# Half-array tiles for every attention product: a windowed attention and an MoE layer on one core

## The chip, the core and the metric

The kernel runs on one core of a Trainium2 chip. Five engines work side by side, each with its own queue, in the order in which the program lists their instructions: TensorE (PE in the profile; its weight loads are shown as PEld) multiplies matrices into PSUM, VectorE (DVE) and ScalarE (ACT) do the element work and empty PSUM, GpSimd (POOL) only clears buffers here, and SyncE (SP) issues the DMAs. Engines wait for each other through semaphores. The metric is the device time of one execution in microseconds (us); lower is better.

## The reference

There are 8 batches of 8 heads with head size 64. Each head has 512 local queries and 32 global ones. A local query sees the 32 global keys and the local keys at most 32 places away; a global query sees all 544 keys. The outputs of the heads, side by side, are the rows of a matrix of 4608 x 512, which goes through two products with a squared ReLU between them. All numbers are float32.

```python
    s_g = scale * np.matmul(q_g, k_all.transpose(0, 1, 3, 2))
    out_g = np.matmul(sm(s_g), v_all)
    s_ll = np.where(mask, s_ll, -1000000000.0)      # mask: |i - j| <= 32
    s_l = np.concatenate([s_lg, s_ll], axis=-1)
    out_l = np.matmul(sm(s_l), np.concatenate([v_g, v_l], axis=2))
...
    h = np.maximum(x @ w_in, 0.0)
    return (h * h @ w_out).astype(np.float32)
```

## The kernel before

**Steps.** The work is cut into 128 half heads `t` (8 batches, two halves of the 512 local queries, 8 heads) and 17 blocks of 256 rows of the MoE layer, each block in 8 steps `m`. One loop over `t` runs both: in pass `t` the attention of half head `t` and the MoE step `m = t - LAG` with `LAG = 9`. From pass 137 on there is MoE work alone. A profile line of nearly every instruction is L52, the line of the helper `InOrder` that records it; tiles' names tell them apart. `InOrder` keeps an engine's instructions in the order of the program from the pass that `FREE` names (17 for DVE, ACT and PE); before that pass the Tile scheduler chooses.

**Precision.** The MoE layer and the half heads from 16 on must keep nearly float32 precision while using the type fp32r, so operands are split into a high part (rounded to fp32r by an ACT copy) and the rest (a DVE subtraction), and a product is the sum of three: high x high, high x low, low x high. Those are `x_h, x_l`, `ws` (weights), `gh, gl`, `hi, lo` (keys, queries and values), `ph, pl` (probabilities). The first 16 half heads and the first MoE block are "plain": unsplit float32 products.

**Attention of a half head.** `load_head` brings one packed tile `raw` with keys, queries and values. Each array row pair holds the head's 64 dimensions twice, so that `scores` can use all 128 rows: rows 0 to 63 hold high parts and rows 64 to 127 low parts of the keys, and two products per query tile give the three terms. `softmax1` (DVE: mask, row maximum), `softmax2` (ACT: two exponentials) and `softmax3` (DVE: reciprocal, scaling) make the probabilities of two query tiles of 128 queries by 224 keys. `transposes` turns them by four 128-wide PE transposes into one PSUM bank `pt`; `pt_split` (four ACT copies) and `pt_rest` (three DVE subtractions) make `ph` and `pl`; `av` multiplies them with the values in nine products of 64 output columns into `xa`; `x_evac` writes `x_h` (ACT) and `x_l` (DVE).

**Global attention.** `g_scores` adds one product per half head for the 32 global queries; for each pair of heads the `jobs` table places softmax, transposes (`g_tr`, into `gt`), the split and 13 products (`g_av`, into `gxo`).

**MoE step.** `gemm1(m, 0)` and `gemm1(m, 1)` are 24 products of 256 columns into the PSUM tile `h`, `act1` is a ReLU on ACT and a square on DVE (`r`), `act2` splits it into `gh` (ACT) and `gl` (DVE), and in the next pass `gemm2(m-1)` is 12 products of 512 columns into `o0` and `o1`. When a block is complete, `evac` copies both with ACT into `ot`, from which they are stored, and the next block starts to write `o0` and `o1`. PSUM has 8 banks: two for `h` in turn, two for `o0, o1`, one each for `s`, `pt`, `xa`, `gs`.

**The order of a pass**: transposes of `t-1`; scores of `t`; first half of gemm1; on ACT `pt_split(t-1)`; softmax1 and softmax2 of `t`; `pt_rest(t-1)`; `evac`; second half of gemm1; `av(t-1)`; `g_scores(t)`; `softmax3(t)`; `act1`; `x_evac`; `split_head(t+1)`; gemm2 of `m-1`; `act2`. So DVE finds `pt_rest` between the mask work and `softmax3`, and `x_l`, `lo` and two `hi` subtractions between the square and `gl`.

## Time and profile before

| | |
|---|---|
| runs of the kernel | 1084.47, 1085.22, 1085.70 us (median 1085.22) |
| profiled execution, first to last instruction | 1083.8 us |
| busy: PE, PEld, DVE, ACT | 98%, 87%, 83%, 67% of the span |
| granted TensorE clock | 0.999 |
| one batch in the middle (16 passes, 339.2 to 463.2 us) | 124.0 us, with DVE busy 111.59 and ACT 87.88 |
| HBM | 86.51 MB read, 8.91 MB written |

The profile shows one execution. Its span is 1.4 us below the median of the runs, so sums made against the span are raised by 1.4 us for the runs. Ends of matmuls are modelled and overlap, so the duration of a row does not say what the matmul costs in a stream; the distance between the starts of two rows does. A batch has two half heads of eight heads and comes back every 124.0 us from about 178 us to about 960 us; before that lies the start with the weights' arrival and the plain heads, after it MoE work alone.

### The profile page before, as it was taken

To read this page: it belongs to the slowest core of one execution; us is meant where nothing else is said; L and a number is where in the kernel's file an instruction comes from. 1 tells how busy PE (TensorE), PEld (TensorE's weight loads), DVE (VectorE), ACT (ScalarE), POOL (GpSimd) and SP (SyncE) were. 2 spreads that over 40 slices of the span, in tenths; PEclk is the share of its full clock that TensorE was granted. 3 is DMA by queue.
4 is the path that set the end of the run, shared out by engine and by line. 5 is a ranking of instruction groups with operands and counts; after the bars stand their busy time and mean duration, and the time that the engine had idled before them with its cause. 6 is when DMAs were issued, how large, how long until landed. Compare 5 with 4: busy or idle time off the path is not lost.

```text
span 1083.8 us, 21401 instructions
## 1 busy us (share of the span) xinstructions
PE 1064.4 (98%) x7648; PEld 941.8 (87%) x7648; DVE 894.2 (83%) x2765; ACT 730.4 (67%) x1887; POOL 2.9 (0%) x10
## 2 busy tenths in 40 slices
PE   7999999999999999999999999999999999999998
PEld 5766789998999899988899989998999889998887
DVE  4689998999889898898989899898989899884322
ACT  5889767767677766767677776767677676773322
POOL 0000000000000000000000000000000000000000
PEclk9999999999999999999999999999999999999999
DMA  9933222222222231322222222222222222211000
GB/s 350 357 138 141 82 81 77 87 70 84 82 79 72 84 93 54 100 73 92 62 88 77 76 78 81 77 88 82 81 72 82 68 97 64 86 31 43 2 20 20
DMA packets 55770, 96.81 MB, mean 89 GB/s; under 512 B 6384, under 2 KB 30704, under 8 KB 55664
## 3 DMA queue, kind: packets, MB, share of 16 engines
q1 hardware_dynamic: 55664, 95.44, 27.1%
q8 instruction: 61, 1.00, 0.4%
q14 instruction: 45, 0.37, 0.1%
HBM read 86.51 MB, written 8.91 MB: 88 GB/s over the span
## 4 chain that ended last, share of the span: by engine, by line
PE 83%; DVE 9%; ACT 5%; issue 1%; DMA 1%; SPq 0%; ACTq 0%
PE o L52 31%; PE h L52 31%; PE xa L52 7%; PE s L52 5%; PE pt L52 5%; PE gxo L52 2%; PE gs L52 2%; DVE prob L52 2%; PE gt L52 1%; DVE ph L52 1%; ACT ph L52 1%; ACT prob L52 1%; DVE ws L52 1%; ACT ws L52 1%; DVE st L52 1%
## 5 line engine op out<-in xcount | busy, mean ns | idle before, releaser
L52 PE MATMUL h<-x_h,ws 128*128 128x256 f32 x2048 | 389.3, 283 | 0.0
L52 PEld LDWEIGHTS h<-x_h,ws 128*128 128x128 f32 x2048 | 327.2, 191 | 0.6
L52 PE MATMUL o<-ws,gh 128*128 128x512 f32 x1024 | 321.3, 395 | 0.0
L52 PE MATMUL h<-x_l,ws 128*128 128x256 f32 x1024 | 289.2, 282 | 0.1
L52 PEld LDWEIGHTS o<-ws,gh 128*128 128x128 f32 x1024 | 185.4, 188 | 34.7
L52 PE MATMUL o<-ws,gl 128*128 128x512 f32 x512 | 202.5, 395 | 0.0
L52 PEld LDWEIGHTS h<-x_l,ws 128*128 128x128 f32 x1024 | 196.0, 191 | 0.8 <-DVE x_l L52 0.4
L52 ACT CAST ph<-pt 128x256 fp32r<-128x256 f32 x448 | 141.1, 341 | 57.9 <-PE pt L52 48.7
L52 ACT ACTIVATE prob<-prob,st 128x224 f32<-128x224 f32 x270 | 127.7, 476 | 75.0 <-DVE st L52 72.4
L52 ACT ACTIVATE r<-h 128x512 f32<-128x512 f32 x136 | 81.5, 600 | 100.5 <-PE h L52 99.5
L52 DVE TENSOR_TENSOR r<-h,r 128x512 f32<-128x512 f32 x128 | 88.6, 692 | 63.4 <-ACT r L52 60.8
L52 PEld LDWEIGHTS o<-ws,gl 128*128 128x128 f32 x512 | 96.2, 188 | 22.9
L52 DVE CUSTOM_DVE_ANT_0 prob<-s,con 128x224 f32<-128x224 f32 x256 | 89.8, 387 | 30.9 <-PE s L52 23.7
L52 ACT CAST hi<-raw 128x864 fp32r<-128x864 f32 x112 | 102.4, 915 | 1.3
L52 DVE TENSOR_TENSOR gl<-r,gh 128x512 fp32r<-128x512 f32 x128 | 88.1, 688 | 12.0 <-ACT gh L52 9.9
L52 PE MATMUL xa<-ph,hi 128*64 128x128 f32 x448 | 89.2, 239 | 1.8 <-DVE ph L52 1.2
L52 ACT CAST gh<-r 128x512 fp32r<-128x512 f32 x128 | 79.1, 618 | 16.0 <-DVE r L52 14.7
L52 DVE TENSOR_TENSOR hi<-raw,hi 64x352 fp32r<-64x352 f32 x224 | 82.6, 369 | 6.9
L52 DVE TENSOR_TENSOR ph<-pt,ph 64x128 fp32r<-64x128 f32 x224 | 79.7, 356 | 7.0
L52 PE MATMUL pt<-con,prob 128*128 128x128 f32 (+1 forms) x512 | 79.5, 278 | 0.0
L52 DVE TENSOR_TENSOR lo<-raw,hi 128x448 fp32r<-128x448 f32 x112 | 69.6, 621 | 7.1 <-ACT hi L52 2.7
L52 DVE TENSOR_SCALAR prob<-prob,st 128x224 f32<-128x224 f32 x242 | 70.6, 334 | 4.1
(76 smaller groups left out, 1549.5 us busy)
## 6 DMA issues: line engine op xcount, KB each, us to landing
raw<-in_pk_dram SPq DMA_DIRECT2D x127, 432.0 KB, 3.2
wr<-in_w_dram SPq DMA_DIRECT2D x32, 512.0 KB, 7.3
gv<-in_vg_dram SPq DMA_DIRECT2D x32, 320.0 KB, 3.6
out_dram<-ot SPq DMA_DIRECT2D x32, 256.0 KB, 2.1
qr<-in_qg_dram SPq DMA_DIRECT2D x28, 64.0 KB, 2.7
out_dram<-ot SPq DMA_DIRECT2D x8, 64.0 KB, 1.7
raw<-in_pk_dram SPq DMA_DIRECT2D x1, 304.0 KB, 2.9
con<-in_consts_dram SPq DMA_DIRECT2D x1, 288.0 KB, 4.7
```

The lines of the kernel that those rows point to most:

```text
L52: r = method(*args, **kwargs)
```

## The change

**Half-array tiles.** Keys and queries of the two query tiles are packed into the two halves of the rows: rows 0 to 63 hold the queries of tile 0 with its 224 keys, rows 64 to 127 those of tile 1. Every score product, probability transpose and global transpose now uses 64 rows of the array, and two such instructions, one per half, follow each other and write to different banks (`sb0, sb1` and `pt0, pt1`). The value products use all rows and 64 of the columns: two heads follow each other, and write to the two halves of the partitions of `xa`.

**Unsplit values.** `av` is float32 without a split: three products per half head, issued for two half heads every second pass. `ph`, `pl`, the three DVE subtractions and three of the four ACT copies are gone; `pt_evac` is one copy of 256 columns on ACT (`pt0`) and one on DVE (`pt1`). `split_head` splits 352 columns in place of 864, in one ACT copy and one DVE subtraction. `x_evac` works on 128 partitions every second pass.

**Global attention for four heads at once**, float32 unsplit: ten transposes, four copies out of PSUM, ten products, where two pairs of heads had ten transposes, 26 products and the splits. The score columns of the global queries now lie in the score banks, and are copied and added on 32 partitions in two or three pieces for each half head.

**Order.** PE keeps the written order from the first pass (`FREE`). In a pass, `av` of a pair, global products, `transposes(t-1)` and the scores of `t+1` come first, then all of gemm1 and gemm2. On DVE and ACT, `softmax3(t)` and `split_head(t+2)` come ahead of the mask work of `t+1`. The tile `h` has one bank.

The core of the diff (DRAM layouts, the removed functions and lines that only follow are left out):

```diff
-FREE = (17, 17, 17)
+FREE = (17, 17, 0)
...
-    ps_h = ctx.enter_context(tc.tile_pool(name="ps_h", bufs=2, space=PSUM))
+    pp = ctx.enter_context(tc.tile_pool(name="pp", bufs=3))
+    ps_h = ctx.enter_context(tc.tile_pool(name="ps_h", bufs=1, space=PSUM))
...
     def load_head(t):
...
+        raw = pq.tile([P, QK], F32, tag="raw", name=f"raw{t}")
+        v = pv.tile([P, VC], F32, tag="v", name=f"v{t}")
+        nc.sync.dma_start(raw, qk[t])
+        nc.sync.dma_start(v, vv[t])
+        heads[t] = dict(raw=raw, v=v)
...
-    pt = ps_a.tile([P, 512], F32, name="pt")
-    nc.vector.memset(pt[96:, 256:], 0.0)
+    sb = [ps_a.tile([P, 512], F32, name=f"sb{u}") for u in range(2)]
+    pt = [ps_a.tile([P, 512], F32, name=f"pt{u}") for u in range(2)]
+    xa = ps_a.tile([P, 512], F32, name="xa")
+    for x in pt:
+        nc.vector.memset(x[96:, 128:256], 0.0)
...
+    def half(u):
+        return slice(64 * u, 64 * u + 64)
...
     def split_head(t):
         if plain(t):
             return
+        hd = heads[t]
+        hi = p2.tile([P, QK], F32R, tag="hi", name=f"hi{t}")
+        lo = p2.tile([P, QK], F32R, tag="lo", name=f"lo{t}")
+        ac.copy(hi, hd["raw"])
+        ve.tensor_sub(lo, hd["raw"], f(hi))
         hd["hi"], hd["lo"] = hi, lo
...
     def scores(t):
         hd = heads[t]
+        hd["s"] = sb
+        if ahead(t) and t % 2:
+            hd["s"] = [ps_o.tile([P, 512], F32, tag=f"o{u}", name=f"s{t}_{u}") for u in range(2)]
+        if plain(t):
+            mm = [(hd["raw"], hd["raw"])]
+        else:
+            mm = [(hd["hi"], hd["hi"]), (hd["hi"], hd["lo"]), (hd["lo"], hd["hi"])]
+        for n, (q, k) in enumerate(mm):
+            for u in range(2):
+                r = half(u)
+                pe.matmul(
+                    hd["s"][u][:, :WIN], q[r, WIN:], k[r, :WIN], start=n == 0, stop=n == len(mm) - 1, skip_group_check=True
+                )
+    def g_scores(t):
+        hd, qz, h4 = heads[t], state["q", t // 4], t % 4
+        for n in range(1 if plain(t) else 2):
+            for u in range(2):
+                r, ks = half(u), slice(32, 160 + 32 * u)
+                o = hd["s"][u][:, WIN : WIN + 128 + 32 * u]
+                if plain(t):
+                    pe.matmul(o, qz[r, :], hd["raw"][r, ks], start=True, stop=True, skip_group_check=True)
+                elif n == 0:
+                    pe.matmul(o[:64], qz[r, h4], hd["hi"][r, ks], start=True, stop=False, skip_group_check=True)
+                else:
+                    pe.matmul(o[:32], qz[r, h4, :32], hd["lo"][r, ks], start=False, stop=True, skip_group_check=True)
+    def g_parts(t):
+        h4, grp = t % 4, (t // 4) % 2
+        s = heads[t]["s"]
+        if (t // 8) % 2 == 0:
+            parts = ((0, 0, 0, 128), (1, 0, 128, 160))
+        else:
+            parts = ((0, 0, 288, 128), (1, 0, 416, 32), (1, 64, 448, 96))
+        r = slice(32 * h4, 32 * h4 + 32)
+        return [(sg[r, grp, d : d + n], s[u][:, WIN + o : WIN + o + n]) for u, o, d, n in parts]
+    def g_copy(t):
+        h4 = t % 4
+        r = slice(32 * h4, 32 * h4 + 32) if plain(t) else slice(32, 64)
+        for dst, src in g_parts(t):
+            ac.copy(dst, src[r])
+    def g_add(t):
+        if plain(t):
+            return
+        for dst, src in g_parts(t):
+            ve.tensor_add(dst, src[:32], dst)
...
     def transposes(t):
         pr = prob[t % 2]
-        for i, (o, n) in enumerate(((0, 128), (320, 128), (128, 96), (224, 96))):
-            pe.transpose(pt[:n, 128 * i : 128 * i + 128], pr[:, o : o + n], ident)
+        for i, (o, n) in enumerate(CHUNKS):
+            for u in range(2):
+                r = half(u)
+                pe.transpose(pt[u][:n, 64 * i : 64 * i + 64], pr[r, o : o + n], ident[r, r])
+    def pt_evac(t):
+        pts = pp.tile([P, 4, P], F32, tag="pts", name=f"pts{t}")
+        ac.copy(pts[:, :, :64], pt[0][:, :256].rearrange("p (c n) -> p c n", c=4))
+        ve.tensor_copy(out=pts[:, :, 64:], in_=pt[1][:, :256].rearrange("p (c n) -> p c n", c=4))
+        heads[t]["pts"] = pts
+    def av(t):
+        pair = [heads[t], heads[t + 1]]
+        for i in range(3):
+            for e, hd in enumerate(pair):
+                v, pts, o = hd["v"], hd["pts"], xa[half(e), :HALF]
+                if i == 0:
+                    pe.matmul(o, v[:96, 128:192], pts[:96, 2:4, :], start=True, stop=False, skip_group_check=True)
+                else:
+                    u = i - 1
+                    pe.matmul(
+                        o[:, P * u : P * u + P],
+                        v[:, half(u)],
+                        pts[:, u, :],
+                        start=False,
+                        stop=i == 2,
+                        skip_group_check=True,
+                    )
+    def x_evac(t):
+        g, c = t // 8, (t % 8) // 2
+        x = xa[:, :HALF]
+        if g == 0:
+            ac.copy(xg[:, c, :], x)
+        else:
+            ac.copy(x_h[:, g % 2, c, :], x)
+            ve.tensor_sub(x_l[:, g % 2, c, :], x, f(x_h[:, g % 2, c, :]))
+        heads[t] = heads[t + 1] = None
...
+    def g_tr(t):
+        s = sg[:, (t // 4) % 2, :]
         for c in range(5):
+            for u in range(2):
+                r = half(u)
+                o = pt[u][:, 256 + 64 * c : 320 + 64 * c] if c < 4 else sb[u][:, 384:448]
+                pe.transpose(o, s[r, 128 * c : 128 * c + 128], ident[r, r])
+    def g_evac(t):
+        gp = p1.tile([P, 5, P], F32, tag="gp", name=f"gp{t}")
+        ac.copy(gp[:, :4, :64], pt[0][:, 256:].rearrange("p (c n) -> p c n", c=4))
+        ve.tensor_copy(out=gp[:, :4, 64:], in_=pt[1][:, 256:].rearrange("p (c n) -> p c n", c=4))
+        ac.copy(gp[:, 4, :64], sb[0][:, 384:448])
+        ve.tensor_copy(out=gp[:, 4, 64:], in_=sb[1][:, 384:448])
+        state["gp"] = gp
+    def g_av(t):
+        gv, gp = state["gv"], state["gp"]
+        for c in range(5):
+            for u in range(2):
+                pe.matmul(
+                    xa[half(u), HALF : HALF + P],
+                    gp[:, c, half(u)],
+                    gv[:, u, c, :],
+                    start=c == 0,
+                    stop=c == 4,
+                    skip_group_check=True,
+                )
+    def g_xs(t):
+        xs = p2.tile([P, P], F32, tag="qr", name=f"gxs{t}")
+        ac.activation(out=xs, in_=xa[:, HALF : HALF + P], func=AF.Copy, scale=state["gst", t][:, 0:1])
...
+    def begin(t):
+        scores(t)
+        g_scores(t)
+    def rise(t):
+        softmax1(t)
+        softmax2(t)
...
     for t in range(NSTEP + LAG + 1):
         m = t - LAG
         ve.on, ac.on, pe.on = [t >= x for x in FREE]
+        prev, run, live, more = 1 <= t <= NT, 0 <= m < NSTEP, t < NT, t + 1 < NT
+        pair = t - 3 if t % 2 and 3 <= t <= NT + 1 else None
+        if t + 4 < NT:
+            load_head(t + 4)
+        if t % 4 == 0 and t + 4 < NT:
+            g_load(t + 4)
         if run:
             w_need(m)
+        if pair is not None:
+            av(pair)
+            x_evac(pair)
+        run_jobs(t, "av")
+        run_jobs(t, "tr")
         if prev:
             transposes(t - 1)
+        if more:
+            begin(t + 1)
         if run:
             gemm1(m, 0)
+            gemm1(m, 1)
         if prev:
+            pt_evac(t - 1)
+        run_jobs(t, "evac")
         if live:
+            softmax3(t)
+        if t + 2 < NT:
+            split_head(t + 2)
+        if more:
+            rise(t + 1)
         if 0 < m <= NSTEP and m % 8 == 1 and m > 8:
             evac(m // 8 - 1)
         w_tick(t, 0)
+        if more:
+            g_copy(t + 1)
+            g_add(t + 1)
+        run_jobs(t, "soft")
+        if t % 4 == 2 and t + 2 < NT:
+            g_split(t + 2)
+        w_tick(t, 1)
         if run:
             act1(m)
+        run_jobs(t, "late")
         if live and t % 4 == 3 and (t // 8) % 2 == 1:
+            d = t if t % 8 == 3 else t + 1
+            e = d + 4 if d % 2 else d + 5
+            for at, place, job in (
+                (d + 1, "soft", g_soft),
+                (d + 1, "soft", g_exp),
+                (d + 2, "soft", g_norm),
+                (d + 2, "late", g_load_v),
+                (d + 3, "tr", g_tr),
+                (d + 3, "evac", g_evac),
+                (e, "av", g_av),
+                (e, "evac", g_xs),
+                (max(e, 17), "late", g_x),
             ):
+                jobs.setdefault((at, place), []).append((job, t))
         if m == NSTEP:
             for i in range(2):
                 gemm2(m - 1, 0, (i,))
                 evac(NBLK - 1, (i,))
         elif m > 0:
             gemm2(m - 1, 0)
             gemm2(m - 1, 1)
         if run:
             act2(m)
         w_tick(t, 2)
```

Three places in the engines' queues carry the steps below. First DVE in one plain pass before: `st` are the row statistics of the softmax, `prob` the probabilities, `r` the square, `gl` the low part that ends the pass.

```order
L52 TENSOR_TENSOR pl_3791<-pt,ph_3790 128x256
L52 TENSOR_TENSOR ph_3790<-pt,ph_3790 64x128
L52 TENSOR_TENSOR ph_3790<-pt,ph_3790 64x256
L52 TENSOR_SCALAR st_3796<-st_3796 128x2
L52 RECIPROCAL st_3796<-st_3796 128x2
L52 TENSOR_SCALAR prob_93<-prob_93,st_3796 128x224 x2
L52 TENSOR_TENSOR r_3839<-h_3777,r_3839 128x512
L52 TENSOR_TENSOR x_l<-xa_3823,x_h 64x256
L52 TENSOR_TENSOR lo_3845<-raw_3669,hi_3844 128x448
L52 TENSOR_TENSOR hi_3844<-raw_3669,hi_3844 64x352
L52 TENSOR_TENSOR hi_3844<-raw_3669,hi_3844 32x64
L52 TENSOR_TENSOR gl_3865<-r_3839,gh_3864 128x512
```

Three subtractions stand where ACT computes the exponentials, and four instructions stand between `r` and `gl`, where ACT computes `gh`. The same engine in one pass of the change, from the end of the mask work to the next:

```order
L53 TENSOR_SCALAR st_5056<-st_5056 128x2
L53 TENSOR_TENSOR sg<-sb_110,sg 32x128
L53 TENSOR_TENSOR sg<-sb_111,sg 32x32
L53 TENSOR_TENSOR sg<-sb_111,sg 32x96
L53 TENSOR_TENSOR r_5068<-h_5020,r_5068 128x512
L53 TENSOR_TENSOR gl_5084<-r_5068,gh_5083 128x512
L53 COPY pts_5136<-pt_113 128x4x64
L53 TENSOR_SCALAR st_5056<-st_5056 128x2
L53 RECIPROCAL st_5056<-st_5056 128x2
L53 TENSOR_SCALAR prob_108<-prob_108,st_5056 128x224 x2
L53 TENSOR_TENSOR lo_5144<-raw_4900,hi_5143 128x352
L53 ISA prob_109,st_5147<-sb_110,con 128x224
```

Between `st` and the `sg` additions, which need ACT's exponentials and copies, nothing stands any more, and nothing between `r` and `gl`. Second, ACT at the end of a block, before:

```order
L52 CAST ph_3790<-pt 128x256
L52 CAST ph_3790<-pt 64x128
L52 CAST ph_3790<-pt 32x256 x2
L52 ACTIVATE prob_93,st_3796<-prob_93,st_3796 128x224 x2
L52 COPY ot_0_3805<-o_3_2999 128x512
L52 COPY ot_1_3808<-o_3_3000 128x512
L52 ACTIVATE r_3839<-h_3777 128x512
```

and with the change:

```order
L53 COPY pts_3726<-pt_112 128x4x64
L53 CAST hi_3733<-raw_3491 128x352
L53 ACTIVATE prob_109,st_3737<-prob_109,st_3737 128x224 x2
L53 COPY ot_0_3743<-o_3_2972 128x512
L53 COPY ot_1_3746<-o_3_2973 128x512
L53 COPY sg<-sb_110 32x128
L53 COPY sg<-sb_111 32x32
```

The copies that free `o0` and `o1` stand behind the exponentials in both, but those now belong to scores whose mask work has `softmax3` and `lo` ahead of it on DVE. Third, PE where the global products are done, with the change:

```order
L53 MATMUL xa<-pts_9439,v_8862 64x256
L53 MATMUL xa<-pts_9533,v_8969 64x256
L53 MATMUL xa<-pts_9439,v_8862 64x128
L53 MATMUL xa<-pts_9533,v_8969 64x128
L53 MATMUL xa<-pts_9439,v_8862 64x128
L53 MATMUL xa<-pts_9533,v_8969 64x128
L53 MATMUL xa<-gv_9353,gp_9442 64x128 x10
L53 MATMUL pt_112<-con,prob_108 128x64
```

The ten global products (`gv`, `gp`) write the same tile `xa` as the pair of half heads just ahead of them, and wait until `x_evac` has read it.

More of the change, by code (lines that the diff above doesn't have):

```diff
@@ L121, in split_head @@
+    nc.gpsimd.memset(sg[:, :, 544:], 0.0)
+    for x in pt:
+        nc.vector.memset(x[96:, 128:256], 0.0)
+    def half(u):
+        return slice(64 * u, 64 * u + 64)
     def split_head(t):
[L123 to L124 removed]
         if plain(t):
             return
[L127 to L130 removed]
@@ L138, in scores @@
-        s = pool.tile([P, 2, WIN], F32, tag=tag, name=f"s{t}")
-        for u in range(2):
-            qs, ks = slice(KC + u * P, KC + u * P + P), slice(128 * u, 128 * u + WIN)
-            if plain(t):
-                pe.matmul(s[:, u, :], hd["raw"][:, qs], hd["raw"][:, ks], start=True, stop=True)
-            else:
-                pe.matmul(s[:, u, :], hd["hi"][:, qs], hd["hi"][:, ks], start=True, stop=False)
-                pe.matmul(s[:, u, :], hd["lo"][:, u * P : u * P + P], hd["hi"][:, ks], start=False, stop=True)
@@ L198, in pt_split @@
-    def pt_split(t):
-        hd = heads[t]
-        if plain(t):
-            pts = p2.tile([P, 512], F32, tag="gh", name=f"pts{t}")
-            ac.copy(pts, pt)
-            hd["pts"] = pts
-            return
-        ph = p1.tile([P, 640], F32R, tag="ph", name=f"ph{t}")
-        pl = p1.tile([P, 256], F32R, tag="pl", name=f"pl{t}")
-        ac.copy(ph[:, :256], pt[:, :256])
-        ac.copy(ph[:64, 256:384], pt[:64, 320:448])
-        for r in (0, 32):
-            ac.copy(ph[r : r + 32, 384:640], pt[64:96, 256:512])
-        hd["ph"], hd["pl"] = ph, pl
@@ L278, in g_load @@
-        state["qz"] = qz
-    def g_scores(t):
-        hd = heads[t]
-        h4 = t % 4
-        if h4 % 2 == 0:
-            state["gs"] = ps_a.tile([P, 288], F32, tag="gs", name=f"gs{t}")
-        kk = hd["raw" if plain(t) else "hi"]
-        pe.matmul(
-            state["gs"],
-            state["qz"][:, 128 * h4 : 128 * h4 + 128],
-            kk[:, 32:320],
-            start=h4 % 2 == 0,
-            stop=h4 % 2 == 1,
-        )
-    def g_evac(t):
-        grp, pair = (t // 4) % 2, (t % 4) // 2
-        gs = state["gs"]
-        early = plain(t)
-        parts = ((0, 0, 288),) if (t // 8) % 2 == 0 else ((288, 0, 160), (448, 192, 96))
-        parts = [(sg[64 * pair : 64 * pair + 64, grp, d : d + n], slice(o, o + n)) for d, o, n in parts]
-        for dst, cols in parts:
-            ac.copy(dst, gs[:64, cols] if early else gs[64:, cols])
-        for dst, cols in parts if not early else ():
-            ve.tensor_add(dst, gs[:64, cols], dst)
@@ new lines, in g_split, with g_load_v @@
+        qr = state["q", t // 4]
+        qz = p2.tile([P, 4, 64], F32R, tag="qz", name=f"qz{t}")
+        q4 = qr.rearrange("p (h n) -> p h n", h=4)
+        ac.copy(qz[:, :, :32], q4)
+        ve.tensor_sub(qz[:, :, 32:], q4, f(qz[:, :, :32]))
+        state["q", t // 4] = qz
+    def g_load_v(t):
+        gv = p1.tile([P, 2, 5, P], F32, tag="gv", name=f"gv{t}")
+        for pair in range(2):
+            src = vg[t // 16, 2 * ((t // 4) % 2) + pair]
+            nc.sync.dma_start(gv[:, pair], src.rearrange("(c p) n -> p c n", p=P))
+        state["gv"] = gv
@@ L394, in w_abs @@
         if i == WCH - 1:
-            wf[i] = p2.tile([P, 512], F32, tag="raw", name=f"wf{i}")
+            wf[i] = p2.tile([P, 512], F32, tag="ot", name=f"wf{i}")
         elif i % 2 == 0:
@@ L561, in w_done, with run_jobs @@
             w_free(i)
-    g_load(0)
-    for t in range(4, 8):
-        load_head(t)
-        if t == 4:
-            w_start(0)
-    scores(0)
+    def run_jobs(t, place):
+        for job, *args in jobs.pop((t, place), ()):
+            job(*args)
+    def begin(t):
[4 more added lines that the diff above has]
+        softmax2(t)
+    g_load(0)
+    w_start(0)
+    begin(0)
+    rise(0)
+    g_copy(0)
     jobs = {}
@@ L600, in attention_moe @@
         w_tick(t, 0)
-        if live and early:
-            g_scores(t)
-        if run:
-            gemm1(m, 1)
-        if prev:
-            av(t - 1)
-        if live and not early:
-            g_scores(t)
-        if early and t + 1 < NPLAIN:
-            scores(t + 1)
-        if live and not early:
-            softmax3(t)
+        if more:
[4 more added lines that the diff above has]
+            g_split(t + 2)
```

255 lines of the change are left out of this document (43 added, 212 removed).

## The prediction, written before the change was timed

> **What bounds the kernel now.** I read the page's busy times first, then one batch by itself in the view by stretches, the waits inside it, and the PE timeline of one pass.
>
> ```profile
> PE 1064.4 (98%) x7648; PEld 941.8 (87%) x7648; DVE 894.2 (83%) x2765; ACT 730.4 (67%) x1887; POOL 2.9 (0%) x10
> ```
>
> ```profile
> 30.10:111.80 81.70, 81.50 (x367) 56.42 (x366) 66.51 (x184) 69.44 (x164) 0.55 (x1) 1.00 0.54 202
> 339.20:463.20 124.00, 123.17 (x938) 111.94 (x937) 111.59 (x351) 87.88 (x233) 0.00 (x0) 1.00 0.26 80
> ```
>
> ```profile
> ACT prob L52 <- DVE st L52: 8.7, 9, 1.9
> ...
> DVE r L52 <- ACT r L52: 2.0, 5, 0.5
> ...
> PE s L52 <- ACT ph L52: 0.6, 1, 0.6
> ...
> PE xa L52 <- DVE ph L52: 0.2, 1, 0.2
> ```
>
> The columns of the stretches are length, then busy time of PE, PEld, DVE, ACT and POOL; in the last fence the waits of that batch, as total, count and longest. PE is busy for 123.17 of 124.00 us and waits under 1 us for DVE and ACT together; the DMA share is 0.26. So PE ends last. But DVE, at 111.59, is 10% behind. A plain pass on PE, by starts:
>
> ```profile
> 443.58 0.22 PE L52 MATMUL xa<-ph,hi 128*64 128x128 f32 x1
> ...
> 444.18 0.30 PE L52 MATMUL gs<-hi,qgz 128*128 128x288 f32 x1
> 444.32 0.62 PE L52 MATMUL o<-ws,gh 128*128 128x512 f32 x2
> ...
> 447.12 0.60 PE L52 MATMUL pt<-con,prob 128*128 128x128 f32 x4
> 447.47 0.35 PE L52 MATMUL s<-hi 128*128 128x224 f32 x1
> 447.66 0.28 PE L52 MATMUL s<-hi,lo 128*128 128x224 f32 x1
> 447.77 0.27 PE L52 MATMUL s<-hi 128*128 128x224 f32 x1
> ...
> 447.99 0.29 PE L52 MATMUL h<-x_h,ws 128*128 128x256 f32 x1
> 450.87 0.22 PE L52 MATMUL xa<-ph,hi 128*64 128x128 f32 x1
> ```
>
> Value products take 0.60 us, the global score 0.14, gemm2 2.80, transposes 0.35, scores 0.52 (0.11 from one to the next), gemm1 2.88: 7.29 us. Sixteen such passes are 116.6; the other 7.4 us of a batch are its global transposes and products.
>
> **PE after the change, plain pass.** The MoE part stays at 5.68. No row before shows two half tiles at once, so each pair is bounded: side by side it costs one matmul, in turn two. Scores: three pairs at 0.11, 0.33 or 0.67. Global scores: two pairs of half the 0.14 row, 0.14 or 0.28. For transposes of 64 columns and for the price of changing the tile's height there are rows:
>
> ```profile
> 509.38 0.40 PE L52 MATMUL o<-ws,gl 128*128 128x512 f32 x1
> 509.70 0.52 PE L52 MATMUL gt<-con,sg 64*128 64x64 f32 x5
> 510.16 0.33 PE L52 MATMUL pt<-con,prob 128*128 128x128 f32 x1
> ```
>
> Gemm2's 12 products take 2.80, 0.23 each, but the step from `o` to `gt`, a 64-row tile, takes 0.32: 0.09 more. The five transposes take 0.46 with a change back, so about 0.37/5, 0.07 each; at best, for half of the 0.35/4 that a 128-column one takes, 0.05. I take 0.06: four pairs, 0.25 or 0.50. Two changes of height a pass, sometimes three: 0.2 to 0.3, I take 0.25. Value products are now float32:
>
> ```profile
> L52 PE MATMUL h<-xg,wf 128*128 128x256 f32 x128 | 30.1, 379 | 0.0
> ```
>
> Those 128 records are 64 products (two records each), so 0.47 us per 256 columns. A half head has 256 + 128 + 128 columns: 0.9 us, and two heads side by side 0.45 each. So value products go from 0.60 to 0.45 or 0.90. The pass is 5.68 + 0.33 + 0.14 + 0.25 + 0.25 + 0.45 = 7.10 side by side, and 5.68 + 0.67 + 0.28 + 0.50 + 0.25 + 0.90 = 8.28 in turn.
>
> The Trainium skill ("TensorE: Matmul & The Clock Gate", Part 3) says that tiles on different strips of the array run concurrently, about 4 ns apart, and measured 2.38 times for three column tiles. No run here shows it; by it the pass is 7.1, and at 2.38/3 of full overlap about 7.5.
>
> I take side by side, at 7.10: the two members of a pair share neither rows and bank, nor, for the values, columns. That is only 0.19 less than before.
>
> **DVE and ACT, plain pass.** The removed work was on these two, some 2 us per pass on DVE, and it was cover. DVE had three subtractions to do while ACT made exponentials, and four while ACT made `gh`. With the change the two engines alternate. Since each keeps program order, the pass cannot be shorter than their chain. Its rows:
>
> ```profile
> 395.63 0.39 DVE L52 CUSTOM_DVE_ANT_0 prob<-s,con 128x224 f32<-128x224 f32 x1 [0.73 <-PE s L52]
> ...
> 398.68 0.17 DVE L52 TENSOR_SCALAR st<-st 128x2 f32<-128x2 f32 x1
> ...
> 399.71 0.69 DVE L52 TENSOR_TENSOR r<-h,r 128x512 f32<-128x512 f32 x1
> ```
>
> ```profile
> 396.58 0.48 ACT L52 ACTIVATE prob<-prob,st 128x224 f32<-128x224 f32 x1
> ...
> 397.43 0.19 ACT L52 ACTIVATION_READ_ACCUMULATOR prob<-prob,st 128x1 f32 x1
> ```
>
> ```profile
> L52 DVE TENSOR_TENSOR gl<-r,gh 128x512 fp32r<-128x512 f32 x128 | 88.1, 688 | 12.0 <-ACT gh L52 9.9
> L52 ACT ACTIVATE r<-h 128x512 f32<-128x512 f32 x136 | 81.5, 600 | 100.5 <-PE h L52 99.5
> L52 ACT CAST gh<-r 128x512 fp32r<-128x512 f32 x128 | 79.1, 618 | 16.0 <-DVE r L52 14.7
> L52 DVE TENSOR_SCALAR prob<-prob,st 128x224 f32<-128x224 f32 x242 | 70.6, 334 | 4.1
> L52 DVE TENSOR_TENSOR hi<-raw,hi 64x352 fp32r<-64x352 f32 x112 | 58.5, 523 | 3.5
> L52 DVE TENSOR_TENSOR pl<-pt,ph 128x256 fp32r<-128x256 f32 x112 | 47.1, 421 | 2.2 <-ACT ph L52 1.2
> L52 DVE STREAM_TRANSPOSE xg<-gxs 32x32 f32<-32x32 f32 x128 | 25.8, 202 | 4.8 <-ACT gxs L52 2.5
> L52 ACT COPY ot<-o 128x512 f32<-128x512 f32 x34 | 18.5, 589 | 3.6 <-PE o L52 3.0
> L52 ACT ACTIVATE sg<-sg,gst 128x544 f32<-128x544 f32 x16 | 11.9, 745 | 0.3 <-DVE gst L52 0.3
> L52 DVE TENSOR_REDUCE gst<-sg 128x1 f32<-128x544 f32 x16 | 11.5, 720 | 0.7 <-ACT sg L52 0.3
> L52 ACT COPY sg<-gs 64x160 f32<-64x160 f32 x32 | 9.2, 288 | 1.8 <-PE gs L52 1.1
> ```
>
> In order: the copy of `pt1`, 256 columns out of PSUM, for which no copy stands in the rows. As many columns in a subtraction out of PSUM (`pl`) take 0.42; the scaling of 224 columns of `prob` takes 0.33. Those are the ends, and I take 0.42, since `pl` shares source and size. `softmax3` 1.03 (398.68 to 399.71). `lo`, 352 columns as in the `hi` row, 0.52. The mask work 0.95 (395.63 to 396.58). Exponentials 1.04 (396.58 to 397.62). Copies of the score columns, two or three on ACT, each at or under the 0.29 of 160 columns: 0.5. ReLU 0.60, square 0.69 (the 399.71 row), `gh` 0.62, `gl` 0.69. `x_l` every second pass, 0.42 as `pl`, so 0.21. That is 7.27. A handoff between engines adds a little and an overlap of neighbours on one engine takes a little; neither has a row of its own, so I take 7.2 with bounds of 7.0 and 7.4.
>
> So the plain pass becomes 7.2, set by PE and the chain almost equally: a gain of 0.09, or 1.4 us per batch. And no engine has slack left for what comes irregularly.
>
> The Trainium skill ("TensorEngine Tiling (Array Packing)", PSUM Bottleneck) warns that tiling speeds up TensorE but not the emptying of PSUM, which can become the bottleneck. That is the direction of my sum; no run here shows it yet.
>
> **What comes irregularly, per batch.**
> - End of a block, twice: `o0` must be copied before gemm2 writes it. PE arrives 0.25 + 0.33 + 0.14 + 2.88 + 0.1 = 3.7 after its transposes start. ACT has the copy done after 0.42 + 1.03 + 0.52 + 0.95 + 1.04 + 0.59 = 4.5, counted from the copy of `pt1`. That starts 0.35 (transposes done) to 2 us (the square just in time for the single bank of `h`) after the transposes; take 1.1. PE waits 4.5 + 1.1 - 3.7 = 1.9, bounds 1.1 and 2.8: 4 us. Before, this copy was hidden. gemm2, and all after it on PE, queue behind.
> - Global products, twice: they wait for `x_l` of the pair just ahead, which stands behind `gl` of the pass before. By the same 1.1, with bounds of 0.3 and 2, and `x_h` and `x_l` in series, 1.5 us: 3 us, with the next transposes and scores queued behind.
> - Their PE work, twice: 5 pairs of transposes at 0.06, 5 pairs of float32 products of 128 columns at 0.23, changes 0.2: 1.6 us, so 3.2 (6 in turn).
> - Global softmax, twice: maximum 0.72 on DVE and exponential 0.75 + 0.19 on ACT come ahead of the ReLU, 1.8 us with the small ones. PE notices when `h` is not free, after about 0.9 us of slack: 0.9 to 1.8, take 1.2: 2.4.
> - The eight 32x32 transposes (1.6, less the 0.6 in which `gl` waits anyway), the copies of the global transposes and the query split add some 3 us to the chain; I count half, 1.4.
>
> Together 14.0 against 7.4 before: +6.6, less 1.4, is +5.2 per batch. From about 112 us (block 1) to 960 us there are 110 passes, 6.9 batches: +36 us. The last 120 us hold MoE work alone and stay.
>
> **Start.** Beside the attention, DVE rounds the weights there:
>
> ```profile
> L52 DVE SCALAR_TENSOR_TENSOR wf<-wr,wf 128x512 int32<-128x512 int32 x32 | 22.1, 690 | 0.6
> L52 DVE TENSOR_SCALAR wf<-wf 128x512 int32<-128x512 int32 x32 | 13.9, 435 | 7.3 <-ACT wf L52 6.9
> raw<-in_pk_dram SPq DMA_DIRECT2D x127, 432.0 KB, 3.2
> ```
>
> Block 0 is bound by PE (81.50 of 81.70 busy). Plain heads lose about half of their float32 products, at 0.47 per 256 columns some 1.2 us per pass for eight passes: -10. But the nine passes ahead of block 0 took 30.1 us, and now each holds `softmax3`, mask work and exponentials in series (3.0), the copy (0.4) and a pass of the weights on DVE (0.44 + 0.69 = 1.1): 4.5, so 40 us: +10. PE keeps written order there, so one block end and one global wait come on top: +8 in all, bounds -10 and +20. The loads shrink (128 rows of 352 and of 192 numbers, 272 KB per half head in two DMAs, for 432 KB in one); at a DMA share of 0.26 that moves nothing.
>
> The sum: 1083.8 + 36 + 8 = 1128 for the profile, 1129 for the runs.
>
> **Rivals.**
> *In turn* (or nearly): if half tiles do not overlap, PE sets the pass at 8.28, (8.28 - 7.29) x 16 = 15.8 per batch; global work 6 and about 3.5 of waits, since a later PE waits less, make 9.5 against 7.4. +18 per batch, 124 in all, and at the start 0: 1208. If only the column tiles fail, 7.55 per pass and about 1160. For it: no row shows overlap. Against: nothing is shared. Chance 0.18.
> *Faster*: the irregular waits vanish in slack. If the chain is 6.9 or less (copies near 0.30, every overlap of 0.08 taken) and PE 7.0, PE gains 0.29 x 16 = 4.6 per batch, and waits fall to about half, 14.0 - 5.4 = 8.6: -3.4 per batch, -23, and with -5 at the start 1056 to 1080, say 1068. It decides once the plain pass falls under 7.29 by more than the growth of the irregular part, 6.6/16 = 0.4, or that growth shrinks with it. Against: the order of DVE lists no cover. Chance 0.20.
> *No effect*: the shorter pass and the waits cancel within a few us, 1080 to 1090. Chance 0.06, two thirds of it within 0.2%.
> My forecast has 0.56, with its own range 1092 to 1165.
>
> A measurement here tells 0.2% (2 us) from no change. Faster 0.20 + 0.01 = 0.21, within 0.2% 0.04, slower 0.56 + 0.18 + 0.01 = 0.75. The range runs from 1068, the middle of the faster case, to 1212, just above the case in turn.
>
> **What would show it.** In the waits of the new profile: PE `o` behind ACT at each block's start, about 2 us; PE `xa` behind DVE `x_l` twice a batch; DVE `gl` behind ACT `gh` and DVE `sg` behind ACT in every pass, 0.6 and 1.4 us. Two `sb` or `pt` rows should start within 0.02 us of each other if tiles overlap, 0.06 to 0.11 apart if not. A plain pass should take 7.2, a batch 129. PE busy without waits and passes near 6.9 would make the chain wrong; passes over 8 would make the overlap wrong.

## The result, and the profile after

| | before | changed |
|---|---|---|
| median of the runs | 1085.37 us (1084.47 to 1085.70) | 1134.78 us (1134.39 to 1137.75) |
| profiled execution | 1083.8 us | 1135.9 us |
| start to the 17th MoE step | 185.41 us | 204.12 us |
| the next 96 steps (six batches) | 744.09 us | 776.67 us |
| one batch | 124.0 us | 129.4 us |
| from there to the end | 154.30 us | 155.11 us |

The changed kernel is slower: 1.0461 times the time before, 95% interval 1.0446 to 1.0476. The forecast was 1129 us, in a range of 1068 to 1212. Of the 52.1 us between the two profiled executions, 32.6 lie in the six batches and 18.7 in the start. A step is counted here from the first `h` product of an MoE step to that of the next.

First the page: busy times, and the granted clock in 40 slices.

```profile
PE 1052.2 (93%) x8320; PEld 878.9 (77%) x8320; DVE 669.6 (59%) x2340; ACT 552.6 (49%) x1617; POOL 0.5 (0%) x5
...
PEclk9798989999999999999999999999999999999999
```

PE was 98% busy before and is 93% busy now, though DVE fell from 894 to 670 us and ACT from 730 to 553. The work that went was off the path; what came is idle time of PE. The clock row is new as well: before it was 9 in every slice, now three slices of the start are at 7 and 8.

Two batches in the view by stretches, the six batches, then two short stretches (length, busy PE, PEld, DVE, ACT, POOL, granted clock, DMA share, GB/s):

```profile
492.73:623.25 130.52, 123.16 (x1022) 104.33 (x1020) 79.51 (x288) 63.89 (x195) 0.00 (x0) 0.97 0.19 56
623.25:752.12 128.87, 121.52 (x1024) 103.17 (x1021) 79.48 (x288) 63.87 (x195) 0.00 (x0) 0.99 0.20 56
...
204.12:980.79 776.67, 732.48 (x6122) 621.21 (x6120) 476.98 (x1729) 383.23 (x1165) 0.00 (x0) 0.98 0.19 56
...
502.38:505.79 3.41, 3.41 (x36) 2.86 (x32) 1.06 (x5) 1.01 (x3) 0.00 (x0) 0.50 0.10 28
533.10:536.51 3.41, 3.32 (x8) 2.64 (x9) 1.80 (x7) 2.48 (x7) 0.00 (x0) 0.50 0.42 159
```

The waits of the first of them (total, count, longest):

```profile
DVE sg L53 <- ACT sg L53: 24.1, 16, 2.3
...
DVE gl L53 <- ACT gh L53: 9.6, 14, 0.7
...
PE o L53 <- ACT ot L53: 3.3, 2, 2.3
PE xa L53 <- DVE x_l L53: 3.2, 2, 2.3
PE h L53 <- DVE r L53: 0.8, 1, 0.8
```

DVE and ACT wait for each other in nearly every pass, as forecast: 9.6/14 = 0.7 us for `gh`, and 24.1/16 = 1.5 us for the score copies that stand behind the exponentials. PE waits in three places only, for 7.3 us. The chain that ended last shows how such a wait comes about, from the global softmax of one pass to the copies that free `o0` and `o1` (start, length, piece):

```profile
524.60 0.73 DVE gst L53
...
526.41 0.60 ACT r L53
...
527.04 0.70 DVE r L53
527.77 0.63 ACT gh L53
528.42 0.69 DVE gl L53
529.11 0.34 DVE pts L53
...
530.34 0.43 DVE lo L53
...
532.02 0.65 ACT prob L53 x3
532.67 0.48 ACT ot L53
...
533.19 4.57 PE o L53 x12
```

For over 8 us the work goes to and fro between DVE and ACT, and PE stands still from 530.92 to 533.19. On the PE timeline, this wait, the one for the global products, and two plain passes:

```profile
501.94 2.02 PE L53 MATMUL xa<-gv,gp 128*64 128x128 f32 x20 [2.28 <-DVE x_l L53]
...
511.46 0.45 PE L53 MATMUL pt<-con,prob 64*128 64x64 f32 x8
511.72 0.35 PE L53 MATMUL sb<-hi 64*128 64x224 f32 x2
511.91 0.28 PE L53 MATMUL sb<-lo,hi 64*128 64x224 f32 x2
512.02 0.28 PE L53 MATMUL sb<-hi,lo 64*128 64x224 f32 x2
...
518.20 1.09 PE L53 MATMUL xa<-pts,v 96*64 96x256 f32 x12
519.22 0.45 PE L53 MATMUL pt<-con,prob 64*128 64x64 f32 x8
...
525.98 0.45 PE L53 MATMUL pt<-con,prob 64*128 64x64 f32 x8
...
533.19 1.22 PE L53 MATMUL o<-ws,gh 128*128 128x512 f32 x2 [2.27 <-ACT ot L53]
```

From transposes to transposes, the pass that ends with the values of two heads takes 519.22 - 511.46 = 7.76 us and the next one 6.76: 7.26 on average. Each row of scores holds both halves (x2): the two members start 0.003 us apart in the trace, and the third pair starts 0.11 us after the second, as one full-array product did before. So the halves run side by side.

### The profile page after: what moved, and what is told of

Its sections match the earlier page's. It is cut to its first block, busy times and chain, and to the rows that moved or that the text cites. A ratio compares the mean times of both kernels' runs of the same rounds, so it can differ in the third digit from the quotient of the medians.

```text
span 1135.9 us, 21870 instructions
## 1 busy us (share of the span) xinstructions
PE 1052.2 (93%) x8320; PEld 878.9 (77%) x8320; DVE 669.6 (59%) x2340; ACT 552.6 (49%) x1617; POOL 0.5 (0%) x5
## 4 chain that ended last, share of the span: by engine, by line
PE 53%; DVE 23%; ACT 14%; issue 4%; DMA 4%; SPq 0%; ACTq 0%; DVEq 0%
PE o L53 22%; PE h L53 19%; PE xa L53 6%; DVE prob L53 6%; ACT prob L53 5%; PE sb L53 3%; DVE gl L53 3%; DVE r L53 3%; ACT gh L53 2%; PE pt L53 2%; DVE st L53 2%; DVE lo L53 2%; ACT r L53 2%; ACT sg L53 2%; DMA wr<-in_w_dram 2%
## 5 line engine op out<-in xcount | busy, mean ns | idle before, releaser
L53 PE MATMUL h<-x_h,ws 128*128 128x256 f32 x2048 | 400.8, 289 | 6.1 <-DVE r L53 6.1
L53 PE MATMUL o<-ws,gh 128*128 128x512 f32 x1024 | 326.2, 400 | 25.7 <-ACT ot L53 25.7
L53 ACT ACTIVATE prob<-prob,st 128x224 f32<-128x224 f32 x256 | 121.3, 475 | 259.9 <-DVE st L53 259.7
L53 DVE TENSOR_TENSOR sg<-sb,sg 32x128 f32<-32x128 f32 (+3 forms) x280 | 60.1, 257 | 159.5 <-ACT sg L53 159.3
L53 DVE CUSTOM_DVE_ANT_0 prob<-sb,con 128x224 f32<-128x224 f32 x248 | 86.4, 386 | 9.4 <-PE sb L53 9.1
L53 DVE COPY pts<-pt 128x256 f32<-128x256 f32 x128 | 53.5, 418 | 40.5 <-PE pt L53 40.0
L53 ACT COPY pts<-pt 128x256 f32<-128x256 f32 x128 | 47.5, 371 | 60.0 <-PE pt L53 59.0
L53 PEld LDWEIGHTS xa<-pts,v 128*64 128x64 f32 (+1 forms) x768 | 47.5, 141 | 35.8 <-issue 24.1
L53 PEld LDWEIGHTS pt<-con,prob 64*128 64x128 f32 (+1 forms) x1024 | 42.3, 137 | 41.5 <-issue 27.5
L53 PE MATMUL xa<-pts,v 128*64 128x128 f32 (+1 forms) x768 | 73.9, 327 | 0.2 <-ACT pts L53 0.2
L53 PE MATMUL pt<-con,prob 64*128 64x64 f32 (+1 forms) x1024 | 61.7, 242 | 8.0 <-DVE prob L53 7.9
```

The costliest lines, as they stand in the source:

```text
L53: r = method(*args, **kwargs)
```

## The experiments

All are compared with the kernel before, run on the same chip. Its median lies between 1085.37 and 1086.14 us each time, so differences from the changed kernel, which did not run beside them, are good to about 2 us. The first four stand on the idle time that the view by lines puts ahead of two groups of PE instructions (last column):

```profile
L53 PE MATMUL o<-ws,gh 128*128 128x512 f32 x1024 | 326.2, 400 | 25.7 <-ACT ot L53 25.7
L53 PE MATMUL xa<-gv,gp 128*64 128x128 f32 x320 | 27.8, 336 | 28.6 <-DVE x_l L53 28.6
```

### The copies of o0 and o1 ahead of the exponentials

```diff
         run_jobs(t, "evac")
+        if 0 < m <= NSTEP and m % 8 == 1 and m > 8:
+            evac(m // 8 - 1)
         if live:
             softmax3(t)
...
             rise(t + 1)
-        if 0 < m <= NSTEP and m % 8 == 1 and m > 8:
-            evac(m // 8 - 1)
```

> Edit: the two copies that free o0 and o1 stand on ACT ahead of the scores' exponentials instead of behind them; nothing else moves. Theory (irregular waits, and a half clock behind some of them): in the changed kernel PE waits 25.7 us in all for these copies, and the granted clock is 0.5 for 3.4 to 10.2 us behind some of the waits. Without the wait some 20 to 35 us go, less up to 1.2 us per block by which ACT's exponentials come later: 1100 to 1120 us, and the row of o shows under 5 us of idle time behind ot. Rival (the alternation of DVE and ACT sets every pass, the waits only show it): the time comes back at the next product that needs the two engines, 1130 to 1140 us, with the idle time moved from o to h.

Measured: 1104.76 us, 1.0174 times before (1.0155 to 1.0194), 30 us less than the changed kernel. The idle time went and did not come back at `h`:

```profile
L53 PE MATMUL o<-ws,gh 128*128 128x512 f32 x1024 | 319.1, 392 | 1.0 <-ACT ot L53 1.0
...
L53 PE MATMUL h<-x_h,ws 128*128 128x256 f32 x2048 | 401.9, 289 | 6.3 <-DVE r L53 6.3
```

The group of `h` had 6.1 us of idle time in the changed kernel and has 6.3 here; the wait of the global products grew from 28.6 to 31.0. So this wait was the order of one queue, and not the two engines' pace showing at one place. The time is in the theory's range. More went than the 25.7 us of the wait itself; the run with filled waits below shows a half clock behind waits as a further cost.

### The global products in the other pass

```diff
-            e = d + 4 if d % 2 else d + 5
+            e = d + 5 if d % 2 else d + 4
```

> Edit: the ten global products are issued in the pass after the one without value products, not right behind the value products of a pair, so x_h and x_l of that tile were written a pass earlier. Theory: the 28.6 us that PE waits for x_l go, and with them the half clock behind several of these waits (3.4 us at half speed is up to 1.7 us lost each, seven times): 1095 to 1110 us. Rival (DVE and ACT set the pass): PE waits as long at the next place, in pt, o or h: 1128 to 1138 us.

Measured: 1101.93 us, 1.0148 times before (1.0131 to 1.0165), 33 us less than the changed kernel, for 28.6 us of waits, and in the theory's range:

```profile
L53 PE MATMUL xa<-gv,gp 128*64 128x128 f32 x320 | 21.0, 278 | 0.0
```

The idle time ahead of `o` stayed at 25.8 us, and that ahead of `h` grew by 2 us. The wait was tied to the place, right behind the pair that fills the same tile.

### Both

> Edit: both of the former, copies of o0 and o1 ahead of the exponentials and global products in the other pass. Theory: 54 us of waits go and nearly all stretches of half clock after 150 us; some 10 to 15 us come back as later exponentials: 1065 to 1085 us, level with the kernel before or faster; a batch in the middle takes 121 to 124 us in place of 129.4. Rival (the alternation of DVE and ACT at 7.2 us a pass plus the global work on the two engines sets the batch): no batch under 127 us, 1110 us or more.

Measured: 1066.41 us, 0.9825 times before (0.9809 to 0.9842): both moves together make a kernel that is faster than the one before. Its six batches, and the waits of PE in one batch:

```profile
188.09:912.06 723.97, 716.75 (x6123) 610.72 (x6121) 475.29 (x1729) 382.20 (x1165) 0.00 (x0) 1.00 0.21 60
```

```profile
PE h L53 <- DVE r L53: 1.2, 1, 1.2
```

A batch takes 723.97/6 = 120.7 us, with the clock at 1.00. Sixteen plain passes of 7.26 are 116.2; the 4.5 left are the global work on PE and this one wait. The start fell too: the 17th step comes at 188.1 us instead of 204.1, 2.7 after the kernel before. The theory's time held, and the batch is even a little shorter than its 121 to 124; the two engines' pace does not hold a batch at 127 us or more.

### The waits filled with work

```diff
+    def fill(n, o):
+        for _ in range(n):
+            pe.matmul(o[:64, 384:512], whi[0][:, :64], whi[0][:, :P], start=True, stop=True, skip_group_check=True)
...
+        if any(job is g_av for job, *_ in jobs.get((t, "av"), ())) and m >= 9:
+            fill(24, sb[0])
         run_jobs(t, "av")
...
+            if m % 8 == 1 and m > 8:
+                fill(24, xa)
             gemm2(m - 1, 0)
```

> Edit: 24 needless products of 128 columns, some 1.4 us of PE work, are issued at the two places where PE waits (ahead of the first gemm2 product of a block, and between the value products and the global products); the waits' causes are untouched. What is tested is the half clock alone. If the granted clock falls because the array stood still for 2 us, the filled waits keep it at 1.00: the eight stretches of 3.4 us at 0.50 after 178 us go, each worth up to 1.7 us, and 1115 to 1128 us are left although work was added. If the clock has nothing to do with the waits, the stretches at 0.50 stay and the time is 1135 to 1145 us, since where the wait is shorter than 1.4 us the filling costs time.

Measured: 1133.25 us, 1.0442 times before (1.0424 to 1.0460). The time is not in the theory's range, but the clock did what the theory says:

```profile
201.32:970.66 769.34, 755.15 (x6698) 646.86 (x6696) 476.78 (x1729) 383.19 (x1165) 0.00 (x0) 1.00 0.20 57
488.70:616.93 128.23, 125.86 (x1118) 107.81 (x1116) 79.47 (x288) 63.86 (x195) 0.00 (x0) 1.00 0.20 57
```

In the changed kernel one of its two batches shown above has two stretches of 3.41 us at a clock of 0.50 and takes 130.52 us, the next has one and takes 128.87; the difference is 1.65, about 3.41/2. Here every batch has none and takes 128.23, although some waits are shorter than the 1.4 us of filling and are lengthened by it. With one stretch less, the 128.87 would be 127.2; so filling costs about 1 us a batch, and saves 1.6 to 3.3. The six batches gain 776.67 - 769.34 = 7.3 us. From there to the end, where MoE work is alone at last and some filling stands before no wait, 159.7 us stand against 155.1. The stretches of half clock follow from idle time: shown. The expectation had their size right, eight times 1.65 us or 13.2 in the six batches, but left out what the filling costs: about 1 us in each batch, and 4.6 us behind them.

### The second half behind the first

```diff
-        for n, (q, k) in enumerate(mm):
-            for u in range(2):
+        for u in range(2):
+            for n, (q, k) in enumerate(mm):
...
-        for i, (o, n) in enumerate(CHUNKS):
-            for u in range(2):
+        for u in range(2):
+            for i, (o, n) in enumerate(CHUNKS):
```

> Edit, on the changed kernel: the half tiles of the upper rows stand all behind those of the lower rows (first all scores of sb0, then all of sb1; first the four transposes of pt0, then of pt1), so that no neighbours lie on different rows. The arithmetic is the same. Theory (neighbours on different halves run at once, and PE sets the plain pass): three score steps of 0.11 and four transposes of 0.06 more per pass, 0.57, times about 119 passes that have attention and MoE work is 68 us; a later PE shortens its own irregular waits (54 us in all) and so the half clock behind them, by 20 to 40 us: 1160 to 1185 us, with second halves of a tile starting 0.06 to 0.11 us after each other instead of 0.004. Rival (DVE and ACT set the plain pass, PE has slack there): 1135 to 1145 us. Rival (overlap does not need neighbours): no change.

Measured: 1133.20 us, 1.0433 times before (1.0415 to 1.0450), the same as the changed kernel. The queue of PE lists three products into `sb0` and then three into `sb1`:

```order
L53 MATMUL sb_110<-hi_7124 128x224
L53 MATMUL sb_110<-lo_7125,hi_7124 128x224
L53 MATMUL sb_110<-hi_7124,lo_7125 128x224
L53 MATMUL sb_111<-hi_7124 128x224
L53 MATMUL sb_111<-lo_7125,hi_7124 128x224
L53 MATMUL sb_111<-hi_7124,lo_7125 128x224
```

The trace of the same kernel has them in pairs:

```profile
510.30 0.36 PE L53 MATMUL sb<-hi 64*128 64x224 f32 x2
510.49 0.28 PE L53 MATMUL sb<-lo,hi 64*128 64x224 f32 x2
510.60 0.28 PE L53 MATMUL sb<-hi,lo 64*128 64x224 f32 x2
```

So the two halves run beside each other though the list puts three products of one half ahead of the other's; the members of a pair start 0.012 us apart in place of 0.003. The rival that no neighbours are needed holds, and the edit did not take the overlap away as it was meant to.

### Both members on one half

```diff
     def scores(t):
...
-                r = half(u)
+                r = half(0)
...
     def g_scores(t):
...
-                r, ks = half(u), slice(32, 160 + 32 * u)
+                r, ks = half(0), slice(32, 160 + 32 * u)
```

The same edit stands in `transposes` and `g_tr`.

> Edit, on the changed kernel: both members of each pair of score products, probability transposes, global scores and global transposes read the lower 64 rows, so the second one takes the operands of the first query tile in place of its own: the computation leaves out the second tile's own scores and weights, its instructions and their sizes stay. Sorting the neighbours had changed nothing, with both halves still starting 0.01 us apart; here the second half cannot start beside the first. Theory (side by side is what keeps the plain pass at 7.27): per pass three score steps of 0.11, four transposes of 0.06 and two global steps of 0.06 more, 0.69; times 119 passes 82 us, less 20 to 40 us of irregular waits and half clock that a later PE does not meet: 1175 to 1200 us, the rival of the prediction in which row tiles go in turn. Rival (overlap is worth little, since DVE and ACT set the pass): 1140 to 1155 us.

Measured: 1193.84 us, 1.0997 times before (1.0978 to 1.1015), 59 us more than the changed kernel. A pass without value products:

```profile
505.30 0.68 PE L53 MATMUL pt<-con,prob 64*128 64x64 f32 x8
505.80 0.46 PE L53 MATMUL sb<-hi 64*128 64x224 f32 x2
506.10 0.38 PE L53 MATMUL sb<-lo,hi 64*128 64x224 f32 x2
506.32 0.38 PE L53 MATMUL sb<-hi,lo 64*128 64x224 f32 x2
```

The step from pair to pair is 0.22 us instead of 0.11, the transposes take 0.50 instead of 0.26 (511.46 to 511.72 above), and the pass 7.43 instead of 6.76 (8.45 instead of 7.76 with the values), close to the 0.69 a pass of the theory, whose range holds. That is the rival "in turn" for the row tiles, made real. The irregular waits shrink as it said, to 11.7 and 11.5 us in the six batches, where the changed kernel has 19.8 and 19.4.

### A longer chain

```diff
         ve.tensor_sub(lo, hd["raw"], f(hi))
+        ve.tensor_sub(lo, hd["raw"], f(hi))
```

> Edit, on the changed kernel: the subtraction that makes lo is done twice, 0.5 us more on DVE in every pass with split heads, ahead of the mask work. Theory as predicted (the alternation of DVE and ACT at 7.2 us stands level with PE, no slack): the pass grows by 0.4 to 0.5, 112 passes, 1175 to 1190 us. Rival (PE alone sets the plain pass at 7.27, the two engines have slack in it): only the irregular waits grow, four per batch and 0.5 us each, 14 us and some half clock: 1145 to 1158 us.

Measured: 1198.09 us, 1.1035 times before (1.1018 to 1.1051), 63 us more than the changed kernel for 112 times 0.5 us. PE's waits in the six batches and their sum of times:

```profile
PE o L53 <- ACT ot L53: 31.2, 12, 2.8
PE xa L53 <- DVE x_l L53: 26.2, 12, 2.8
PE h L53 <- DVE r L53: 18.9, 25, 2.4
```

```profile
202.17:1034.94 832.77, 755.31 (x6121) 636.47 (x6121) 525.74 (x1824) 378.73 (x1165) 0.00 (x0) 0.96 0.18 52
```

The changed kernel has 19.8, 19.4 and 5.0 us there. The six batches take 56.1 us more, 0.58 for each of the 96 passes: PE waits 32 us longer, and its busy time grows by 23 us, since the clock falls from 0.98 to 0.96 of the stretch. That is the theory's side, and above its range, which left out the clock; the engine that is 59% busy in the page had almost no slack. But several plain passes keep their 6.75 and 7.75 us on PE here. The chain itself can be read from DVE: from `gl` to `gl`, plain passes in which the two engines wait for each other alone take 7.08 to 7.12 us in the changed kernel (from 432.95 to 440.03 and 447.15 us) and 7.64 to 7.68 here (446.60, 454.25, 461.92). So the chain of the changed kernel lies some 0.15 us below PE's pass of 7.26, and with 0.5 us more it lies above it.

### The first value product on 128 rows

```diff
-                    pe.matmul(o, v[:96, 128:192], pts[:96, 2:4, :], start=True, stop=False, skip_group_check=True)
+                    pe.matmul(o, v[:, 128:192], pts[:, 2:4, :], start=True, stop=False, skip_group_check=True)
```

> Edit, on the kernel with both waits moved (1066.4 us): the first value product of a half head uses all 128 rows (the lower 32 hold zeros in both operands) instead of 96. What it prices is the 0.09 us that the step from o to this product takes above the 0.23 of the steps from o to o. If the change of height from 128 to 96 rows costs it, the step falls to 0.23 and 64 pairs times 0.094 are 6 us: 1060 to 1062 us. If it is something else (the float32 weights), the step stays and the time is 1065 to 1068 us.

Measured: 1064.92 us (1064.32 to 1066.54), 0.9810 times before (0.9795 to 0.9824). The step is unchanged:

```profile
478.56 0.40 PE L53 MATMUL o<-ws,gl 128*128 128x512 f32 x1
478.89 1.09 PE L53 MATMUL xa<-pts,v 128*64 128x256 f32 x12
```

It is 0.33 us with 128 rows as with 96, 0.1 above the 0.23 from `o` to `o`. So the price at this place is not that of a height of 96. The width alone does not explain it either: in the kernel before, the step from `o` to a product of 64 columns with fp32r operands (`gxo`) takes 0.23 us, from 641.55 to 641.78. Whether the float32 type of the value products costs it wasn't tried. The 1.5 us by which the time differs can't be told from none.

### PE's order at the start left to the scheduler

```diff
-FREE = (17, 17, 0)
+FREE = (17, 17, 17)
```

> Edit, on the kernel with both waits moved (1066.4 us): the scheduler chooses PE's order too before pass 17, as in the kernel before. In that kernel the seventeenth MoE step starts at 188.1 us, in the one before at 185.4, so of the start's 18.7 us all but 2.7 went with the two waits. Theory (what the written order costs at the start are waits on DVE for the first probabilities and for the global products, and a free order fills them): 1056 to 1064 us. Rival (the first 46 us are DVE, ACT and the weights' arrival, whatever PE does): 1064 to 1069 us.

Measured: 1065.70 us, 0.9817 times before (0.9803 to 0.9832), no change from the 1066.41, in the rival's range. The first MoE product comes at 23.8 us instead of 46.2, and the ninth step at nearly the same time (122.2 and 123.7). The eight steps stretch from 77.5 to 98.3 us. What bounds this stretch was not tried; it is not the time at which PE begins.

### All together

> Edit: both waits moved, value products on 128 rows, and the scheduler's order of PE before pass 17, all that had not made the time longer. Theory (PE is the bound from the second block on, and the start is bound by the weights' arrival on DVE and ACT): 1063 to 1066 us, the three parts do not add up. Rival (the two small gains of 1.5 and 0.7 us were real and add): 1062 to 1064 us.

Measured: 1062.77 us (1062.21 to 1064.61), 0.9794 times before (0.9779 to 0.9808). It is the fastest of the versions, 3.6 us below the one with the two moves alone. The number is in the rival's range and just below the theory's. Its six batches take 723.80 us, the same as there, and they begin at 184.75 us in place of 188.09: what it gains lies at the start. Which part of the edit gains it was not tried apart from the two runs above.

## Why the prediction was right

**Right: what bounds a pass.** The prediction had PE at 7.10 and the alternation of DVE and ACT at 7.2. Measured are 7.26 on PE and, in passes without a wait for PE, 7.1 for the chain, inside its bounds of 7.0 to 7.4. So the two are nearly equal as forecast, but PE is the longer one. The copy out of PSUM on DVE, for which there was no row, took what was chosen:

```profile
L53 DVE COPY pts<-pt 128x256 f32<-128x256 f32 x128 | 53.5, 418 | 40.5 <-PE pt L53 40.0
```

PE was undersized by 0.16 and the gain per plain pass was 0.03 instead of 0.09. Two rows account for most of it: the first score step takes 0.19 us and not 0.11 (511.72 to 511.91), as it did in the prediction's own rows (447.47 to 447.66), and the values of a pair cost 7.76 - 6.76 = 1.00, or 0.50 a pass instead of 0.45.

**Right: side by side.** The pairs run at once, and the run with both members on one half shows what it would cost otherwise: 59 us. The Trainium skill ("TensorE: Matmul & The Clock Gate", Part 3) says that tiles on different strips run concurrently; the pairs at the distance of one product agree. The prediction's estimate by that section's 2.38 is 0.1 too high: its 1.17 us of paired work over 2.38/3, and the 5.93 of the rest, add to 7.4 us and not to 7.5.

**Right: the two waits.** For a batch the prediction had 4 us for `o` behind `ot` and 3 for `xa` behind `x_l`; the rows say 3.3 and 3.2. Moving the two took the time from 1134.8 to 1066.4. The mechanism named for each (the copies behind the exponentials; `x_l` behind `gl`, with the global products right behind their pair) is the one that the edits removed.

**The sum of a batch came out for a partly other reason.** Forecast were 129.2, measured 129.4; that they meet so closely is luck, as errors of 1 to 4 us cancel. By terms: plain passes 16 x 7.26 = 116.2 where 115.2 stood; PE's global work 3.3 (4.5 in the version with both waits moved, less its 1.2 of wait), where 3.2 stood; the waits 7.3, where 4, 3, 2.4 for the global softmax and 1.4 for the rest stood, 10.8. The global softmax costs 0.8 to 1.2 at `h`, half of what was set, and the rest does not show. In their place stands a term that the prediction did not have: half clock, eight stretches in the six batches, 1.65 us each, 2.2 a batch. 116.2 + 3.3 + 7.3 + 2.2 = 129.0.

**Too small: the start.** The term was +8 with bounds of -10 and +20, for the time to the first step of block 1. That step, the ninth, comes at 132.0 us instead of 120.5, 11.5 later. At the 17th step it is 18.7, where 8 and eight passes of the forecast's growth make 10.6; nearly all of the 8 us by which the profiled time is above the forecast lie here. The 8 is also not the sum of its terms: -10, +10 and one wait of each kind, 1.9 and 1.5, are 3.4. The first `h` does come late, at 45.0 us instead of 30.1, but the runs show that this is made up for: with both waits moved, 46.2 leads to +2.7 only at the 17th step. The other 16 us are mainly waits at the same two places, 12.6 us in all and single ones larger than in a batch, and the clock behind them:

```profile
102.42 2.40 PE L53 MATMUL xa<-gv,gp 128*64 128x128 f32 x20 [5.45 <-DVE x_l L53]
...
138.97 1.22 PE L53 MATMUL o<-ws,gh 128*128 128x512 f32 x2 [3.85 <-ACT ot L53]
```

```profile
90.00:110.00 20.00, 14.55 (x87) 10.73 (x86) 15.08 (x43) 13.15 (x35) 0.00 (x0) 0.83 0.23 64
130.00:150.00 20.00, 13.98 (x104) 10.72 (x105) 11.32 (x39) 9.60 (x25) 0.00 (x0) 0.74 0.15 49
```

Here the weights are still being split on the same two engines: ahead of this `x_l`, at 101.95 us, DVE has six subtractions of weights in a row (3.69 us from 98.34). That `x_l` and `ot` come later because of the weights is read from the queue, and was not tried by a run.

**The rival "faster"** asked for a chain of 6.9 or less and half the waits. The chain was not shorter, but the waits turned out to hang on two places in the order; with these moved, the case came true as another kernel (a batch of 120.7). The prediction treated the waits as a price of the missing cover. They were that, but a price at two places that the order could avoid.

## What to carry to other kernels

Work that is removed from engines off the critical path can still be cover for the waits between two other engines: look what stood between each pair of dependent instructions, and count the chain that is left. Rare work (a block's end, a batch's global part) is then where time is lost, so look at what stands ahead of it in its queue before giving up the change: two small moves turned 4.6% slower into 1.8% faster. After an edit that adds waits to TensorE, read the clock row too: here a wait of 2.3 us could cost 1.65 us more behind it.

## What the runs showed of the hardware

**Half clock after a wait.** A wait of PE of 2.3 us was followed by 3.41 us at a granted clock of 0.50 in some cases (530.92 to 533.19, half clock from 533.10) and not in others:

```profile
664.74:668.15 3.41, 3.41 (x40) 2.48 (x39) 2.04 (x7) 1.66 (x4) 0.00 (x0) 1.00 0.32 122
```

This stretch follows a wait of 2.27 us that ended at 663.59. The stretches of 0.50 begin at 372.68, 502.38, 533.10 and 632.09 us by the clock records, whose distances of 129.70, 30.72 and 98.99 are 38, 9 and 29 times 3.413: they lie on a fixed grid, so it matters where in the grid a wait falls. The wait from 530.92 fills 2.18 us of the window that ends at 533.10. The one from 661.32 to 663.59 lies across the boundary at 662.81, with 1.49 us in one window and 0.78 in the next. So it is in all six batches: in the window ahead of each of the eight stretches PE stood still for 1.89 to 2.28 us by its rows, and for at most 1.49 us in every other window. Two waits of the same length were thus enough, or not, by their place alone. The Trainium skill ("TensorE: Matmul & The Clock Gate", Part 1) describes a clock gate with a free-running window of 3.4 us that goes to half rate after an idle window; grid and half rate agree. But here 1.89 to 2.28 us of standing still were enough, less than a whole window. Products that only keep PE busy during the wait kept the clock at 1.00.

**Halves need not be neighbours.** With three products of one half listed ahead of the three of the other, the halves still ran in pairs, and the time did not change. What decides is that they use different rows: with both on the same rows, the step doubled from 0.11 to 0.22 us.
